# Half of an attention low part moved from VectorE to GpSimd, its scale folded into the exponential, and narrower reuse waits for one tile pool

## The chip, the cores and the metric

The kernel runs on one core of a Trainium2 chip. The metric is the device time of one execution in microseconds (us). The comparison is between the median of several executions of the kernel before and after one change; one further execution of each is profiled.

## The reference

The layer normalizes x, then adds to x an attention block and a mixture of experts that both read the normalized x. All eight experts are taken for every token (K = E = 8), so the gate is a softmax over eight logits.

```python
B, S, D, H = 1, 2048, 448, 16          # attention; Dh = 28
B, S, D, F, E = 1, 2048, 448, 1792, 8  # experts
def _A_ref(x, wqkv, wo):
    q, k, v = ...                                    # (B, H, S, Dh) each
    scores = jnp.einsum("bhqd,bhkd->bhqk", q, k) * (Dh ** -0.5)
    p = _softmax(scores, axis=-1)
    o = jnp.einsum("bhqk,bhkd->bhqd", p, v)
    return ... @ wo
def _B_ref(x, w_gate, w1, w2):
    ...
    for e in range(E):
        h = _silu(xf @ w1[e]) @ w2[e]
        out = out + w * h
xn = _layernorm(x, axis=-1)
return x + _A_ref(xn, A_wqkv, A_wo) + _B_ref(xn, B_w_gate, B_w1, B_w2)
```

## The kernel before, in words

**Numbers as two halves.** Products that need more than one fp16 are done with a value split in two: a high part (the value rounded to fp16) and a low part (the value minus the high part, again fp16). High parts are made on ScalarE (ACT), low parts on VectorE (DVE) or GpSimd (POOL), and TensorE (PE) adds up high times high, high times low and low times high.

**Two streams and one phase ahead of them.** `phase0` normalizes x, makes Q and K (written to the scratch tensor `qk` in DRAM) and V (`vs`). Then two streams run interleaved to the end. `moe` takes 24 groups of expert columns: `hidden` (L1062 and, for the last 64 rows of the contraction, `tails` L1070, four products in quarters of the array) makes z, `silu` makes t = silu on ACT and DVE (L1104, L1107), its high part hh on ACT (L1110) and its low part hl on POOL in two pieces of 256 columns (L1114), and `summed` (L1131) multiplies by the second weight and adds to `acc` on DVE (L1143). The weights' low parts are on POOL as well (L556, L574).

**Attention** takes 16 heads x 16 tiles of 128 queries, each tile in two halves j of 1024 keys, 512 halves in all. For a half, `score` makes the products (L1222) into the one PSUM slot of tag "s", DVE takes the row maximum mx (L1226), `expo` on ACT makes nm = -c mx (L1237, 128x1) and pf = exp(c s + nm) (L1238, f32), and `halves` makes ph = fp16(4096 pf) on ACT (L1247) and pl = 4096 pf - ph on DVE (L1250). `turn` transposes ph and pl by DMA on SP's queue (L1266) into th and tl. Every four tiles `weigh` multiplies tl by V (L1300, four products in column strips of 32) and th by V (L1307); small sums follow on POOL and DVE. Every fourth head `project` multiplies by wo (L1407). The next score product into slot "s" has to wait until the exponential has read the slot: score, maximum, nm, exponential, score is a loop that runs 512 times.

**What sets the order.** `Plan` records jobs with an estimated duration and then places them one by one with a list scheduler: for each engine the job with the lowest due time that is ready by the estimates. The order found is written out as each engine's program, in that order; on the chip each engine and SP's queue take it in order and wait on semaphores. For PE the scheduler ranks down work that has been ready for less than SURE = 2500 ns, and it keeps products in quarters or strips together (KEEP, HOLD), since it counts FORM = 95 ns for entering such a block. A DVE job marked `lock` and a POOL job are counted as excluding each other (SHARED).

**Pools.** `Pools` opens a pool "p0" for the tiles of `phase0`; when the last job that uses it has been placed, it closes p0 and opens "ap" over the same memory, for the attention's tiles (V, K, Q, pf, ph, pl, th, tl and others). In SP's queue the first job of "ap" is the load of head 0's V, then follow the loads of its K and Q.

Of the kernel before, what the change touches and what calls it, by code (L numbers as in the profile page):

```python
# [2 lines left out]

# [6 lines left out]
F32 = mybir.dt.float32  # L10
F16 = mybir.dt.float16
I32 = mybir.dt.int32
AF = mybir.ActivationFunctionType
ALU = mybir.AluOpType
# [4 lines left out]
P = 128  # L19
# [7 lines left out]
C = 512  # L27
# [7 lines left out]
P_SCALE = 4096.0  # L35
# [25 lines left out]
class Plan:  # L61
# [15 lines left out]
    def add(self, eng, ns, fn, v, r=(), w=(), size=0, after=(), lock=False, land=0, form=0, pace=0, rush=False):  # L77
        j = Job()
        j.lock, j.land, j.form, j.pace, j.rush, j.at = lock, land, form, pace, rush, 0
        j.eng, j.ns, j.fn, j.v, j.seq, j.size = eng, ns, fn, v, len(self.jobs), size  # L80
        j.then = []
        deps = set(after)
        for k in r:
            if k in self.wrote:
                deps.add(self.wrote[k])
        for k in w:
            if k in self.wrote:
                deps.add(self.wrote[k])
            deps.update(self.read.get(k, ()))
        for k in r:  # L90
            self.read.setdefault(k, []).append(j)
        for k in w:
            self.wrote[k], self.read[k] = j, []
        j.wait = len(deps)
        for d in deps:
            d.then.append(j)
        j.bufs = []
        for k in (*r, *w):
            b = k[0] if isinstance(k, tuple) else k
            if isinstance(b, Buf) and b not in j.bufs:  # L100
                j.bufs.append(b)
                b.users += 1
        j.many = sum(isinstance(k, Buf) and k.pool == "ps" for k in w) > 1
        j.frees = next((k for k in r if isinstance(k, Buf) and k.pool == "ps"), None) if eng != "PE" else None
        self.jobs.append(j)
        return j
# [204 lines left out]
class Pools:  # L311
# [17 lines left out]
    def issued(self, j):  # L329
        if any(b.pool == "p0" for b in j.bufs):  # L330
            self.left -= 1
            if not self.left:
                self.ctx.__exit__(None, None, None)
                del self.have["p0"]
                self.ctx = self.tc.tile_pool(name="ap", bufs=1)
                self.have["ap"] = self.ctx.__enter__()
                self.have["tl"] = self.ring

# [5 lines left out]
def block_kernel(ctx, tc, x, wqkv, wo, w_gate, w1, w2, out):  # L344
    nc = tc.nc
# [35 lines left out]
    shift = mp.tile([P, NT], F32, name="shift")  # L381
    cexp = mp.tile([P, 1], F32, name="cexp")
    cneg = mp.tile([P, 1], F32, name="cneg")
    sc_o = mp.tile([P, 1], F32, name="sc_o")
    inv_o = mp.tile([P, 1], F32, name="inv_o")

# [789 lines left out]
    def attention(at):  # L1176
# [53 lines left out]
        def expo(i, j, v):  # L1230

            PR[i, j] = p = buf("ap", [P, 2 * C], F32, f"pf{i}_{j}", tag="pf", bufs=RF)
            s, m, n = sc.pop((i, j)), mx[i // NB * NB], i % NB
            nm = buf("ap", [P, 1], F32, f"nm{i}_{j}", tag="nm", bufs=4)

            def powers():
                nc.scalar.activation(nm(), m()[:, n, j : j + 1], AF.Copy, scale=cneg)  # L1237
                nc.scalar.activation(p(), s(), AF.Exp, bias=nm(), scale=cexp)  # L1238

            add("ACT", 1532, powers, v, r=[s, (m, n, j), "cexp"], w=[p, nm])  # L1240

        def halves(i, j, v):
            p = PR.pop((i, j))
            h, l = PF[i, j] = [
                buf("ap", [P, 2 * C], F16, f"p{a}{i}_{j}", tag=f"p{a}", bufs=n) for a, n in (("h", RPH), ("l", RPL))
            ]
            add("ACT", 1052, lambda: nc.scalar.activation(h(), p(), AF.Copy, scale=P_SCALE), v, r=[p], w=[h])  # L1247
            add(
                "DVE", 1212,
                lambda: nc.vector.scalar_tensor_tensor(l(), p(), P_SCALE, h(), op0=ALU.mult, op1=ALU.subtract), v,  # L1250
                r=[p, h], w=[l], lock=True,
            )

        def turn(i, j, v):
            q = i % NB
            if not q and not j:
                PT[i] = [], []
            hs, ls = PT[i - q]
            h, l = PF.pop((i, j))
            if not j:  # L1260
                hs.append(buf("ap", [P, NKT, P], F16, f"th{i}", tag="th_", bufs=TH))
                ls.append(buf("tl", [P, NKT, P], F16, f"tl{i}", tag="tl", bufs=TL))
            th, tl, ks = hs[q], ls[q], slice(j * NKT // 2, (j + 1) * NKT // 2)
            for b, p, out in (((th, j), h, lambda: th()[:, ks]), ((tl, j), l, lambda: tl()[:, ks])):
                add(
                    "SP", 1290, lambda out=out, p=p: nc.sync.dma_start_transpose(out(), p()), v, r=[p], w=[b],  # L1266
                    size=950, land=TURN,
                )

# [151 lines left out]
        for i, (h, t) in enumerate(TILES):  # L1421
            v = at(i)
# [36 lines left out]
YPARTS = (0, 2), (2, 5)  # L1459
SPARE, SPINS, KAT, ONACT, NAT = 9, 6, -500, 'vqk', (-2000, -250, 0, 0)  # L1460
PACE, HOLD, CUT = 3500, 8000, 256
LANDQ, LANDX, SPK = 7500, 8500, -300
TURN, TURN_S, LOAD, MXS, SCM, LK, LQ = 5500, 4500, 4500, 4700, 4600, 3000, 2600
# [23 lines left out]
```

## Time and profile before

| | us |
|---|---|
| median of 3 executions | 2631.62 (2630.65 to 2634.79) |
| the profiled execution's own time | 2626.93 |
| its span, first to last instruction | 2625.1 |
| PE busy | 2609.3 (99%) |
| DVE busy | 2138.0 (81%) |
| ACT busy | 2115.9 (81%) |
| POOL busy | 1380.7 (53%) |

Busy time of an engine is the time in which at least one of its instructions runs. Matmuls overlap, and the end of each is modelled, so a busy PE may still be slower than it could be: the distance between two starts tells its pace. Granted clock 1.00 is 2.4 GHz, and 0.50 is 1.2 GHz. A stage's wait is read in the view of waits, which names who ended an engine's idle time.

### The profile page before, as it was taken

The page shows a single profiled execution, that of the slowest core. Times are in us where ns is not written, and L with a number is a line of the kernel's source. Part 1 is how long each engine was busy: PE and PEld are TensorE (multiplying, and loading weights), DVE is VectorE, ACT ScalarE, POOL GpSimd, SP SyncE. Part 2 cuts the span into 40 slices and gives each one's busy share as a digit, 9 for nine tenths or more (in the row PEclk, how much of TensorE's full clock was granted, in tenths as well). Part 3 has the DMA queues.
Part 4 walks back from the last instruction along what each step waited for, and adds up shares of the span by engine and source line. Part 5 has one row for each costly group of instructions (what it writes and reads, how often), then busy time and mean ns, then how long its engine had stood idle before and what let it go on. Part 6 is the DMA issues. An engine that isn't in the chain of part 4 may idle for free.

```text
span 2625.1 us, 49947 instructions
## 1 busy us (share of the span) xinstructions
PE 2609.3 (99%) x17851; PEld 1283.5 (49%) x17851; DVE 2138.0 (81%) x2832; ACT 2115.9 (81%) x3134; POOL 1380.7 (53%) x1915
## 2 busy tenths in 40 slices
PE   9999999999999999999999999999999999999999
PEld 4444444544445444444454444445444444444544
DVE  8478888788988888888888788978888788877873
ACT  6488898778987889878888788887898788887862
POOL 2255475535654456555546455554565455655542
PEclk9999999999999999999999999999999999999999
DMA  7568888888887888688796787968887788867751
GB/s 233 176 125 160 172 153 145 144 146 154 153 154 147 156 158 169 125 154 152 140 174 120 144 147 145 166 118 149 168 159 129 136 144 159 165 122 132 136 103 63
DMA packets 1221465, 386.84 MB, mean 147 GB/s; under 512 B 1156832, under 2 KB 1203296, under 8 KB 1221216
## 3 DMA queue, kind: packets, MB, share of 16 engines
q1 hardware_dynamic: 1220656, 383.63, 77.2%
q8 instruction: 140, 2.29, 0.4%
q14 instruction: 109, 0.89, 0.1%
q10 hardware_dynamic: 560, 0.02, 0.0%
HBM read 85.11 MB, written 15.23 MB: 38 GB/s over the span
## 4 chain that ended last, share of the span: by engine, by line
PE 93%; DVE 3%; ACT 2%; DMA 1%; issue 1%; SPq 0%; DVEq 0%; ACTq 0%
PE banks L1131 37%; PE banks L1062 34%; PE banks L1222 8%; PE banks L1307 4%; PE banks L893 3%; PE banks L1300 2%; PE banks L1070 2%; PE banks L916 1%; PE banks L1407 1%; DVE mx L1226 1%; DVE pl L1250 1%; ACT pf L1238 0%; DMA tl<-pl 0%; DMA scmg<-mxs 0%; ACT ph L1247 0%
## 5 line engine op out<-in xcount | busy, mean ns | idle before, releaser
L1114 POOL TENSOR_TENSOR hl<-t,hh 128x256 f16<-128x256 f32 x896 | 718.2, 822 | 647.2 <-ACT hh L1110 613.2
L1062 PE MATMUL banks<-xa,w 128*128 128x512 f16 x3136 | 974.9, 380 | 0.0
L1131 PE MATMUL banks<-w,hh 128*128 128x448 f16 x3584 | 970.6, 352 | 1.8 <-DVE t L1107 1.8
L1226 DVE TENSOR_REDUCE mx<-banks 128x1 f32<-128x1024 f32 x512 | 624.2, 1219 | 133.3 <-PE banks L1222 123.4
L1250 DVE SCALAR_TENSOR_TENSOR pl<-pf,ph 128x1024 f16<-128x1024 f32 x512 | 683.9, 1337 | 41.8 <-ACT ph L1247 38.5
L1062 PEld LDWEIGHTS <-w 128*128 128x128 f16 x4480 | 425.8, 97 | 531.3 <-issue 39.6
L1131 PE MATMUL banks<-w,hl 128*128 128x448 f16 x1792 | 631.3, 352 | 0.0
L1238 ACT ACTIVATE pf<-banks,nm,cexp 128x1024 f32<-128x1024 f32 x512 | 616.9, 1205 | 17.1
L1247 ACT ACTIVATE ph<-pf 128x1024 f16<-128x1024 f32 x512 | 538.2, 1051 | 5.6 <-DMA th<-ph 1.2
L1131 PEld LDWEIGHTS <-hh 128*128 128x128 f16 x3584 | 346.3, 98 | 343.5 <-issue 5.4
L1062 PE MATMUL banks<-xb,w 128*128 128x512 f16 x1344 | 509.1, 379 | 0.0
L1107 DVE SCALAR_TENSOR_TENSOR t<-t,banks 128x512 f32<-128x512 f32 x448 | 297.6, 681 | 96.8 <-ACT t L1104 95.5
L1237 ACT ACTIVATE nm<-mx,cneg 128x1 f32<-128x1 f32 x512 | 148.7, 290 | 270.5 <-DVE mx L1226 268.3
L1143 DVE SCALAR_TENSOR_TENSOR acc<-banks,gwe,acc 128x448 f32<-128x448 f32 x384 | 258.9, 678 | 126.3 <-PE banks L1131 125.4
L1104 ACT ACTIVATE t<-banks,the 128x512 f32<-128x512 f32 x448 | 295.3, 681 | 60.9 <-PE banks L1070 38.9
L1110 ACT ACTIVATE hh<-t 128x512 f16<-128x512 f32 x448 | 268.0, 622 | 59.6 <-PE banks L1131 54.3
L1222 PE MATMUL banks<-K,Q 112*128 112x512 f16 x1024 | 306.2, 380 | 4.3 <-DMA K<-qk 2.1
L1131 PEld LDWEIGHTS <-hl 128*128 128x128 f16 x1792 | 174.8, 98 | 164.2
L556 POOL TENSOR_TENSOR w<-r,w 128x256 f16<-128x256 f32 x224 | 176.1, 805 | 101.8 <-ACT w L552 101.8
L574 POOL TENSOR_TENSOR w<-r,w 128x224 f16<-128x224 f32 x224 | 150.4, 691 | 78.2 <-ACT w L571 72.5
L1222 PEld LDWEIGHTS <-Q 112*128 112x128 f16 x1024 | 94.5, 98 | 108.8 <-issue 20.3
L1307 PEld LDWEIGHTS <-th 128*128 128x128 f16 x4096 | 127.2, 96 | 27.9 <-issue 1.3
(154 smaller groups left out, 1839.5 us busy)
## 6 DMA issues: line engine op xcount, KB each, us to landing
r<-in_B_w_dram SPq DMA_DIRECT2D x48, 448.0 KB
r<-in_B_w_dram SPq DMA_DIRECT2D x48, 320.0 KB
th<-ph SPq DMA_TRANSPOSE x512
tl<-pl SPq DMA_TRANSPOSE x512
K<-qk SPq DMA_DIRECT2D x128, 56.0 KB
Q<-qk SPq DMA_DIRECT2D x256, 28.0 KB
r<-in_B_w_dram SPq DMA_DIRECT2D x24, 256.0 KB
r<-in_B_w_dram SPq DMA_DIRECT2D x32, 160.0 KB
```

Source lines behind the costliest of these rows:

```text
L1062: nc.tensor.matmul(z(), rows(w)[:, blk, :], xx, start=(i == 0 and not late), stop=(i == NTERM - 2 and late))
L1104: add("ACT", 680, lambda: nc.scalar.activation(t(), z(), AF.Tanh, scale=th_()[:, 0:1]), v, r=[z, th_], w=[t])
L1107: lambda: nc.vector.scalar_tensor_tensor(t(), t(), 1.0, z(), op0=ALU.add, op1=ALU.mult),
L1110: add("ACT", 620, lambda: nc.scalar.activation(hh(), t(), AF.Copy), v, r=[t], w=[hh])
L1114: nc.gpsimd.tensor_tensor(hl()[:, cs], t()[:, cs], hh()[:, cs], ALU.subtract)
L1131: nc.tensor.matmul(y()[:, 0:D], a, wv, start=(i == 0 and u == 0), stop=(i == g - 1 and u == 2))
L1143: lambda: nc.vector.scalar_tensor_tensor(acc[:, n, :], y()[:, 0:D], gb()[:, n : n + 1], acc[:, n, :], op0=ALU.mult, op1=ALU.add),
L1222: nc.tensor.matmul(b()[:, cs], q()[:, q0 : q0 + P], k()[:, cs], start=True, stop=True)
L1226: "DVE", 1220, lambda: nc.vector.tensor_reduce(m()[:, n, j : j + 1], b(), op=ALU.max, axis=AX.X), v,
L1238: nc.scalar.activation(p(), s(), AF.Exp, bias=nm(), scale=cexp)
L1247: add("ACT", 1052, lambda: nc.scalar.activation(h(), p(), AF.Copy, scale=P_SCALE), v, r=[p], w=[h])
L1250: lambda: nc.vector.scalar_tensor_tensor(l(), p(), P_SCALE, h(), op0=ALU.mult, op1=ALU.subtract), v,
```

## The change

Three things are changed together. nm becomes `Identity(-c mx + log 4096)`, with the constant in a tile `lift` as bias, so that pf comes out multiplied by 4096 and ph is a plain rounding of it. The low part is then pf - ph, a `tensor_tensor`: for the first half of every tile (j = 0) it stays one instruction on DVE, for the second half (j = 1, by `MIX`) it becomes two instructions of 512 columns on POOL (`CUTP`), and the transpose of that half waits for both pieces. And the pool "ap" is opened with `reuse_waits="tile"`: each of its tiles waits only for those users of p0 whose bytes it takes over.

```diff
-                self.ctx = self.tc.tile_pool(name="ap", bufs=1)
+                self.ctx = self.tc.tile_pool(name="ap", bufs=1, reuse_waits="tile")
...
+    lift = mp.tile([P, 1], F32, name="lift")
+    nc.vector.memset(lift, math.log(P_SCALE))
...
-                nc.scalar.activation(nm(), m()[:, n, j : j + 1], AF.Copy, scale=cneg)
+                nc.scalar.activation(nm(), m()[:, n, j : j + 1], AF.Identity, bias=lift, scale=cneg)
                 nc.scalar.activation(p(), s(), AF.Exp, bias=nm(), scale=cexp)
...
-            add("ACT", 1052, lambda: nc.scalar.activation(h(), p(), AF.Copy, scale=P_SCALE), v, r=[p], w=[h])
-            add(
-                "DVE", 1212,
-                lambda: nc.vector.scalar_tensor_tensor(l(), p(), P_SCALE, h(), op0=ALU.mult, op1=ALU.subtract), v,
-                r=[p, h], w=[l], lock=True,
-            )
+            add("ACT", 1052, lambda: nc.scalar.activation(h(), p(), AF.Copy), v, r=[p], w=[h])
+            if (2 * i + j) % MIX[1] not in MIX[0]:
+                add("DVE", 1212, lambda: nc.vector.tensor_tensor(l(), p(), h(), ALU.subtract), v, r=[p, h], w=[l], lock=True)
+                return
+            for k in range(2 * C // CUTP):
+
+                def low(cs=slice(k * CUTP, (k + 1) * CUTP)):
+                    nc.gpsimd.tensor_tensor(l()[:, cs], p()[:, cs], h()[:, cs], ALU.subtract)
+
+                add("POOL", POOL_NS(CUTP), low, v, r=[p, h], w=[(l, k)])
...
+CUTP, MIX = 512, ((1,), 2)
```

The estimate for nm and the exponential together (1532 ns) is left as it was. Since the jobs' engines change, the scheduler finds another order for the whole of the two streams; the number of instructions of PE, ACT's work and the two table loads of ACT stay as they were.

SP's queue before, from the last writes of Q and K by `phase0` (`qk<-qh`, `qk<-ql`) to the first loads of the attention (V0, K0_0 and Q0_0 of head 0), with the semaphores that each row waits for; the program's DMAs raise the eight semaphores DMAHW0 to DMAHW7 in turn as they land, so these make eight groups:

```order
L389 DMA mxs_69<-mxr1_1322 128x2 [waits DMAHW2_49,DVE_49]
L389 DMA qk_68<-qh3_6_1320 128x512 [waits DMAHW3_49,Activation_49]
L389 DMA qk_68<-ql3_6_1328 128x512 [waits DMAHW4_49,DVE_49]
L389 DMA V0_1347<-vs_70 128x1024 [waits DMAHW4_49,DMAHW5_49,DMAHW3_49,DMAHW6_49,DMAHW1_49,DMAHW7_49,DMAHW0_49,PE_49]
L389 DMA K0_0_1353<-qk_68 28x1024 x4
L389 DMA Q0_0_1374<-qk_68 28x512 [waits DMAHW2_49]
L389 DMA Q0_0_1374<-qk_68 28x512 x2
L389 DMA Q0_0_1374<-qk_68 28x512 [waits DMAHW5_49]
```

The same place now:

```order
L392 DMA mxs_69<-mxr1_1324 128x2 [waits DMAHW2_49,DVE_49]
L392 DMA qk_68<-qh3_6_1322 128x512 [waits DMAHW3_49,Activation_49]
L392 DMA qk_68<-ql3_6_1330 128x512 [waits DMAHW4_49,DVE_49]
L392 DMA V0_1349<-vs_70 128x1024 [waits DMAHW5_49]
L392 DMA K0_0_1355<-qk_68 28x1024 [waits DMAHW6_49]
L392 DMA K0_0_1355<-qk_68 28x1024 [waits DMAHW7_49]
L392 DMA K0_0_1355<-qk_68 28x1024 [waits DMAHW0_49]
L392 DMA K0_0_1355<-qk_68 28x1024 [waits DMAHW1_49]
L392 DMA Q0_0_1376<-qk_68 28x512 [waits DMAHW2_49]
L392 DMA Q0_0_1376<-qk_68 28x512 [waits DMAHW3_49]
L392 DMA Q0_0_1376<-qk_68 28x512 [waits DMAHW4_49]
L392 DMA Q0_0_1376<-qk_68 28x512 [waits DMAHW5_49]
```

The order of the rows is the same; the load of V0 waited for seven groups of DMAs and for PE and now waits for one group, and each of the eight loads behind it waits for the previous DMA of its own group, the last write to `qk` (DMAHW4) among them for the third piece of Q0_0.

POOL before, around the first low parts hl of column block 1 of expert group 2, with the small sums of attention tiles 20 to 23 (lw20, u20) between:

```order
L574 TENSOR_TENSOR w2_3_0_4314<-r2_3_3658,w2_3_0_4314 128x224 x2
L1336 TENSOR_TENSOR lw20_4359<-lw20_4359 128x8x29
L1340 TENSOR_TENSOR lw20_4359<-lw20_4359,c20_4155 128x8x29
L1114 TENSOR_TENSOR hl2_0_1_4423<-t2_0_1_4367,hh2_0_1_4411 128x256
L1344 TENSOR_TENSOR u20_4220<-u20_4220,lw20_4359 128x8x29
L1114 TENSOR_TENSOR hl2_0_1_4423<-t2_0_1_4367,hh2_0_1_4411 128x256
```

POOL now, around the same hl:

```order
L1257 TENSOR_TENSOR pl24_1_4359<-pf24_1_4322,ph24_1_4341 128x512 x2
L1117 TENSOR_TENSOR hl2_0_1_4381<-t2_0_1_4336,hh2_0_1_4357 128x256 x2
L559 TENSOR_TENSOR w1_3_4_4238<-r1_3_3299,w1_3_4_4238 128x256 x2
L1117 TENSOR_TENSOR hl2_1_1_4415<-t2_1_1_4352,hh2_1_1_4395 128x256 x2
L1117 TENSOR_TENSOR hl2_2_1_4438<-t2_2_1_4379,hh2_2_1_4426 128x256 x2
L1257 TENSOR_TENSOR pl25_1_4461<-pf25_1_4411,ph25_1_4436 128x512 x2
```

The low parts of attention tiles 24 and 25 (pl24_1, pl25_1), which stood on DVE, stand in POOL's row ahead of and behind the experts' hl.

On PE the order holds blocks of products in quarters or strips (L1070, L1300 before) that are entered from full products: 145 such blocks before, 149 now.

## Rows read from the trace of the kernel before

**Rows 1.** The page's busy time by engine (busy us, share of the span, instructions), the first row of its chain that ended last, and that chain's shares of the span by line, from the view of the chain in order of time.

```profile
PE 2609.3 (99%) x17851; PEld 1283.5 (49%) x17851; DVE 2138.0 (81%) x2832; ACT 2115.9 (81%) x3134; POOL 1380.7 (53%) x1915
...
PE 93%; DVE 3%; ACT 2%; DMA 1%; issue 1%; SPq 0%; DVEq 0%; ACTq 0%
...
by line: PE banks L1131 37.0%; PE banks L1062 34.1%; PE banks L1222 8.2%; PE banks L1307 3.9%; PE banks L893 2.5%; PE banks L1300 2.3%; PE banks L1070 2.1%; PE banks L916 1.3%; PE banks L1407 1.2%; DVE mx L1226 0.9%; issue 0.7%; DVE pl L125
```

**Rows 2.** The view of waits for PE alone, whole span: who waited for whom, us in total, times, longest us.

```profile
PE banks L956 <- DMA acc<-in_A_x_dram: 4.6, 1, 4.6
PE banks L1222 <- DMA K<-qk: 2.1, 1, 2.1
PE banks L1131 <- DVE t L1107: 1.8, 1, 1.8
PE banks L1222 <- ACT pf L1238: 1.7, 3, 1.3
PE banks L956 <- ACT xn L790: 1.0, 1, 1.0
PE banks L1307 <- DMA th<-ph: 0.3, 1, 0.3
```

**Rows 3.** The chain that ended last in order of time, 115 to 137 us: start us, us, what. SPq is SP's queue.

```profile
120.87 3.91 DMA qk<-ql
...
125.05 0.32 SPq L389
...
128.00 0.39 SPq L389
...
128.74 0.31 SPq L389
...
130.53 0.56 DMA K<-qk
131.08 1.00 PE banks L1222 x2
```

**Rows 4.** The view of stretches: from:to in us and length, busy us of PE, PEld, DVE, ACT, POOL (instructions), granted clock of PE, share of DMA, GB/s.

```profile
126.00:131.08 5.08, 2.98 (x15) 1.21 (x14) 0.84 (x2) 2.03 (x4) 3.85 (x6) 1.00 0.50 144
131.08:134.45 3.37, 3.37 (x9) 1.13 (x10) 1.89 (x2) 1.35 (x3) 0.00 (x0) 0.50 0.39 87
134.45:140.00 5.55, 5.55 (x28) 2.28 (x27) 2.87 (x5) 3.79 (x6) 1.30 (x2) 1.00 0.74 184
```

**Rows 5.** The timeline of PE around one block of products in quarters: start us, us, engine, line, operation.

```profile
123.20 0.59 PE L1062 MATMUL banks<-xa,w 128*128 128x512 f16 x2
123.73 0.39 PE L1070 MATMUL banks<-xa,w 64*128 64x512 f16 x1
...
123.96 0.38 PE L1070 MATMUL banks<-xa,w 64*128 64x512 f16 x1
...
124.27 0.39 PE L1062 MATMUL banks<-xa,w 128*128 128x512 f16 x1
124.49 0.38 PE L1062 MATMUL banks<-xb,w 128*128 128x512 f16 x1
```

**Rows 6.** Groups of instructions with shapes kept apart: line, engine, operation, out<-in, shapes, count | busy us, mean ns of one | idle us before them and what ended it. First DVE, then POOL, then ACT.

```profile
L1250 DVE SCALAR_TENSOR_TENSOR pl<-pf,ph 128x1024 f16<-128x1024 f32 x512 | 683.9, 1337 | 41.8 <-ACT ph L1247 38.5 <-ACT c L1313 1.4 <-DMA tl<-pl 1.0
L1226 DVE TENSOR_REDUCE mx<-banks 128x1 f32<-128x1024 f32 x512 | 624.2, 1219 | 133.3 <-PE banks L1222 123.4 <-ACT ph L1247 5.9 <-ACT t L1104 1.2
L817 DVE TENSOR_TENSOR tb<-xn,ta 128x448 f16<-128x448 f32 x8 | 5.0, 621 | 9.8 <-ACT ta L815 9.8
L410 DVE TENSOR_REDUCE mx<-r 128x1 f32<-128x1280 f32 x32 | 47.3, 1477 | 1.8 <-DMA r<-in_B_w_dram 1.8
L410 DVE TENSOR_REDUCE mx<-r 128x1 f32<-128x896 f32 x32 | 34.5, 1079 | 1.9 <-DMA r<-in_B_w_dram 1.9
...
L705 POOL TENSOR_TENSOR WA<-rqk,WA 128x448 f16<-128x448 f32 x4 | 4.1, 1036 | 11.2 <-DMA rwo<-in_A_wo_dram 6.0 <-DMA acc<-in_A_x_dram 5.1
...
L1237 ACT ACTIVATE nm<-mx,cneg 128x1 f32<-128x1 f32 x512 | 148.7, 290 | 270.5 <-DVE mx L1226 268.3
L570 ACT ACTIVATE r<-r,scog 128x448 f32<-128x448 f32 x112 | 73.4, 656 | 0.0
L790 ACT ACTIVATE xn<-acc,shift,rstd 128x448 f32<-128x448 f32 x15 | 10.6, 761 | 7.4 <-DVE tb L817 4.4 <-DVE shift L778 1.0 <-POOL WA L705 1.0
```

**Rows 7.** The views of two lines: the low part pl on DVE, and the experts' low part hl on POOL (durations min/median/max in ns), what hl waited for longest (us, times), and who waited for hl.

```profile
L1250 DVE SCALAR_TENSOR_TENSOR pl<-pf,ph x512: 1209/1224/1790, 138.2 to 2543.7; 128x1024 f16<-128x1024 f32 x171
...
L1114 POOL TENSOR_TENSOR hl<-t,hh x896: 658/671/1766, 126.3 to 2610.7; 128x256 f16<-128x256 f32 x180
...
  ACT hh L1110: 613.2, 199
...
  ACT t L1104: 3.0, 3
```

**Rows 8.** Timelines of ACT and PE where an exponential ends and the next score product starts, at the first and the last of the 44 places (of 511) where less than 0.1 us lies between.

```profile
215.35 1.20 ACT L1238 ACTIVATE pf<-banks,nm,cexp 128x1024 f32<-128x1024 f32 x1
...
216.65 0.60 PE L1222 MATMUL banks<-K,Q 112*128 112x512 f16 x2
...
2451.73 1.21 ACT L1238 ACTIVATE pf<-banks,nm,cexp 128x1024 f32<-128x1024 f32 x1
...
2452.99 0.38 PE L1222 MATMUL banks<-K,Q 112*128 112x512 f16 x1
```

More of the change, by code (lines that the diff above doesn't have):

```diff
@@ L2 @@
 import heapq
+import math
 import concourse.bass as bass
@@ L1265, in turn @@
                 add(
-                    "SP", 1290, lambda out=out, p=p: nc.sync.dma_start_transpose(out(), p()), v, r=[p], w=[b],
+                    "SP", 1290, lambda out=out, p=p: nc.sync.dma_start_transpose(out(), p()), v, r=[p] if p.tag == "ph" else [p, *((p, k) for k in range(2 * C // CUTP))], w=[b],
                     size=950, land=TURN,
```

## Prediction

> **What bounds the kernel now.** I read the busy times first, then the chain that ended last, then the waits of PE, then the one place where PE waits long. PE is busy for 2609.3 of 2625.1 us, and the chain is PE for 93% [rows 1]: nothing can be won here but what PE loses, and the change takes no instruction from PE. The view of waits gives all that PE loses to others: 4.6 + 2.1 + 1.8 + 1.7 + 1.0 + 0.3 = 11.5 us [rows 2]. Of these 4.6 and 1.0 (L956) lie ahead of the two streams, where the change alters nothing. So 5.9 us are left, with what the clock loses behind a wait, against which every new wait counts in full. DVE and ACT stand at 81%, POOL at 53% [rows 1]; what moves between them is worth nothing by itself. Only a wait that reaches PE is.
>
> **The pool's waits.** PE's longest wait in the streams is for the first attention loads: it is idle for 2.10 us until 131.08 [rows 2, 3], so it was ready at 128.98. Right behind it PE is granted 0.50 for 3.37 us, in which it is busy all the time, and 1.00 again after that [rows 4]: at half pace these 3.37 us do the work of 1.69, so 1.7 us go there. The wait and the clock cost 3.8 us together. Why the loads are late is in SP's queue: the last write of `qk` is issued at 120.87 (0.38 long) and lands 3.91 us later, at 124.78; only then V0's load goes, at 125.05 [rows 3], since it waits for all of p0's DMAs, and K0_0 and Q0_0 stand behind it. Now V0 waits for one group of DMAs. At best the whole row of loads moves up to the end of that issue, 121.25, by 3.8 us, and the products could start at 127.3. Against this stands that each load now waits for its own group: the third piece of Q0_0 waits for the write that lands at 124.78. It was issued at 128.00 [rows 3], so it comes 3.2 us earlier, and the products could start at 127.9. Both ends lie ahead of 128.98, so I take the whole 3.8 us off. Next late after that is ordinary work: the scores that follow wait for the slot, not for loads.
>
> **The low part on two engines.** DVE loses 256 instructions of 1337 ns [rows 6], 342 us, and falls to about 1796 us (68%). The 256 that stay become a plain `tensor_tensor`: 621 ns for 448 columns, and 1477 - 1079 = 398 ns more for 384 columns of a reduction, 1.04 a column, give 621 + 576 x 1.04 = 1.22 us [rows 6], the same as the 1224 ns of the old form [rows 7]. POOL gains 512 pieces. A low part of 256 columns takes 671 ns [rows 7], one of 448 takes 1036 [rows 6], 1.90 ns a column; a piece of 512 is then 1036 + 64 x 1.90 = 1158 ns, and 512 of them are 593 us. POOL comes to 1974 us, 75%. None of this lies on PE's path as long as the hl behind the pieces are in time: PE never waited for POOL [rows 2], and POOL idled 613 us in front of hl for want of hh [rows 7]. The transpose of a second half now waits for two pieces in line, 2.3 us where it was 1.2, behind which SP's queue stands; four tiles are weighed together, and PE waited for transposes 0.3 us in all [rows 2]. I cost this part at 0, with its loss among the rivals. The plain rounding of ph costs the same as the scaled one, and `lift` is set once ahead of everything: 0.
>
> **nm with a bias tile.** This term stands on a path. `Identity` with scale and bias tiles takes 761 ns on 448 columns, `Copy` with a scale tile alone 656 [rows 6]: a second tile as operand costs 0.105 us, so nm goes from 290 to about 395 ns, and ACT from 2115.9 to 2170 us (83%), hidden. But nm is in the loop score, maximum, nm, exponential, score, and the planner's estimate doesn't know of it. How often does that loop bind PE? By the chain, DVE's maximum has 0.9% of 2625.1 us, 23.6 us, or 19 maxima of 1219 ns [rows 1, 6]: 19 x 0.105 = 2.0 us. The bounds: 0, if the order found now leaves more room, and 44 x 0.1 = 4.4 us, since at 44 of 511 places the next score starts less than 0.1 us behind the exponential: from 215.35 + 1.20 to 216.65 at the first, from 2451.73 + 1.21 to 2452.99 at the last [rows 8]. I take 2.0, because the chain counts only the loops that had no other slack.
>
> **The new order of PE.** It enters blocks in quarters or strips 149 times, before 145. The second product ahead of such a block starts at 123.20 + 0.22 = 123.42 (full products start 0.22 apart, 124.27 to 124.49), the block at 123.73, 0.31 later; behind it 123.96 to 124.27 is again 0.31 [rows 5]. So a block costs 2 x 0.09 = 0.18 us, and four more 0.7 us. The bounds are 0 (fewer blocks follow straight on another) and 0.7; I take 0.7. The remaining waits in the streams (1.8 for t, 1.7 for the exponential, 0.3) are accidents of one order and will stand elsewhere in the new one; I leave them at their sum.
>
> **The sum.** -3.8 + 2.0 + 0.7 = -1.1 us. The profiled execution took 2626.93 us, 4.7 less than the median of 2631.62; its waits are applied to the median: 2631.6 - 1.1 = 2630.5 us, and with the bounds of nm (0 to 4.4) and the blocks (0 to 0.7) 2627.8 to 2632.9.
>
> **Rivals.** *The waits in the streams go too.* DVE loses 342 us of 2138, and PE's wait for t was one for DVE, so the room could take the 1.8 and the 1.7 away, with nm free: 2631.6 - 3.8 - 3.5 + 0.7 = 2625.0. For it: DVE's maxima start sooner. Against it: ACT gets fuller, and 2 of the 5.9 us hung on it.
>
> *POOL takes the wait's place, slower.* hl stands behind pieces of pl in one row. Two pieces (2.3 us) and one DVE low part that holds the port (1.2 us) delay an hl by 3.5 us; the planner holds some 2.5 us ready for PE (SURE), so 1.0 us of PE is idle each time. POOL and the DVE's remaining low parts together, were they never side by side, are 1974 + 256 x 1.22 = 2287 us, 87% of the span, so this must be a matter of single crowded places. From 7 of them on the kernel is slower by over 0.2%; eight give 2638.5. That the two engines exclude each other is seen in the rows: pl takes 1224 ns as a rule and up to 1790, hl 671 and up to 1766 [rows 7], each less than the other's length more. The Trainium skill (SBUF — State Buffer, "SBUF: two separate sides") calls this an exclusive lock of a port pair that is held for a whole instruction; the trace agrees by these maxima. The Trainium skill (GPSIMD Engine Reference, "Engine selection") speaks against the whole move: it wants two-input elementwise work on VectorE, with GpSimd about 2x slower; the rows say 2 x 1158 against 1224 ns, 1.9x, and it would cost only where POOL is waited for.
>
> *The pool's change does nothing for PE.* V0's load might share its way with the late writes and land no earlier than 3.7 us (125.05 to 128.74, the last piece of Q0_0) behind 124.78; that last piece waits for V0's group. Then the first product stays within 0.3 us of where it was, and 2631.6 + 2.0 + 0.7 = 2634.3 is left. Against it: V0's load would stand 3.8 us ahead in the queue.
>
> **How the numbers follow.** The forecast has 0.50, the waits that go too 0.23, POOL 0.17, the pool's change without effect 0.10. 0.2% is 5.3 us, about what a measurement of this kernel can tell from no change: faster means under 2626.4, slower over 2636.9. Faster: the second case and a little of the first's lower end, 0.25. Slower: POOL's, 0.17. The rest, 0.58, is the same. The range reaches from just under the second case, 2624.5, to 2638.0, which leaves out the worse half of POOL's case and little below; the forecast's own range is 2627.8 to 2632.9.
>
> **What would show it.** Right: PE has no wait near 129 us and its granted clock stays at 1.00 there; nm near 395 ns; the pieces on POOL near 1.16 us and POOL at about 75%, DVE near 68%; small waits of PE for the exponential in greater number. Wrong: rows of PE waiting for POOL's hl, or for the transposes of tl; a wait for K or Q still at 129 us; nm still at 290 ns.

## The result, and the profile after

The changed kernel takes 2653.53 us (median of 5 runs, 2652.06 to 2657.81), the kernel before 2631.16 us beside it (5 runs, 2628.0 to 2634.79). The ratio is 1.0087, 95% interval 1.0076 to 1.0097: the change costs 22.4 us. The forecast was 2630.5 with a range of 2624.5 to 2638.0, so it was wrong: too low by 23 us. It had counted differences of up to 0.2% as no change, and the changed kernel is slower by more than that. The profiled execution has a span of 2650.3 us, 25.2 more than before.

In the lines of the changed kernel the score product is L1225, the maximum mx L1229, nm L1240, the exponential L1241, ph L1250, pl L1252 on DVE and L1257 on POOL, hl L1117, and the transposes L1273.

Busy time by engine after, from the page; it answers to [rows 1]:

```profile
PE 2618.9 (99%) x17851; PEld 1283.1 (48%) x17851; DVE 1862.6 (70%) x2577; ACT 2162.0 (82%) x3134; POOL 1834.7 (69%) x2427
```

No engine but PE is near its limit. PE itself does the same 17851 products and is busy for 9.6 us longer, and its time without work grows by 25.2 - 9.6 = 15.6 us. A product's row lasts 380 ns though full products start 220 ns apart [rows 5], so a start that is late by less than some 160 ns (an estimate, 380 - 220) shows as longer busy time and not as a wait. That small delays stand in the 9.6 us is borne out below, by two runs with the same order of PE (e3 and e6).

Waits of PE after (who waited for whom, us in total, times, longest us); they answer to [rows 2]:

```profile
PE banks L1225 <- ACT pf L1241: 19.3, 27, 3.8
PE banks L959 <- DMA acc<-in_A_x_dram: 4.6, 1, 4.6
PE banks L959 <- ACT xn L793: 1.2, 1, 1.2
PE banks L1134 <- DVE t L1110: 0.5, 1, 0.5
PE banks L1065 <- DVE t L1110: 0.3, 1, 0.3
```

The wait of 2.1 us for K is gone, as forecast, and the wait for t is 0.8 us where it was 1.8. In their place the score waits for the exponential 27 times and 19.3 us; before it was 3 times and 1.7 us [rows 2]. POOL doesn't appear.

Groups of the moved work after (busy us, mean ns of one | idle us ahead of them and what ended it); the DVE and ACT groups of [rows 6] answer to them:

```profile
L1257 POOL TENSOR_TENSOR pl<-pf,ph 128x512 f16<-128x512 f32 x512 | 594.1, 1177 | 240.9 <-ACT ph L1250 162.9 <-DMA tl<-pl 43.5 <-issue 15.7
L1240 ACT ACTIVATE nm<-mx,lift,cneg 128x1 f32<-128x1 f32 x512 | 195.7, 382 | 236.3 <-DVE mx L1229 234.7
```

A piece on POOL takes 1177 ns on the mean and nm 382 ns: the durations came out about as forecast (1158 and 395).

Waits of ACT, then of POOL, after:

```profile
ACT ph L1250 <- POOL pl L1257: 22.0, 11, 4.8
ACT ph L1250 <- DMA th<-ph: 6.0, 3, 4.8
```

```profile
POOL pl L1257 <- DMA tl<-pl: 43.5, 25, 5.5
```

ACT's wait for pl is new, and so is POOL's for tl: before, pl stood on DVE and waited for tl 1.0 us in all [rows 6], and ACT waited in front of ph for this alone:

```profile
ACT ph L1247 <- DMA th<-ph: 1.2, 2, 0.6
```

How such a wait gets to PE is seen at PE's longest one. Timeline after, all engines, 579 to 594 us (start us, us, engine, line, operation, in brackets the idle time ahead of it and who ended it); SPq is SP's queue, where the us of a transpose is its issue:

```profile
579.39 1.06 ACT L1250 ACTIVATE ph<-pf 128x1024 f16<-128x1024 f32 x1 [0.67 <-POOL pl L1257]
...
580.41 1.24 SPq L1273 DMA_TRANSPOSE tl<-pl  x1
...
582.01 1.20 ACT L1241 ACTIVATE pf<-banks,nm,cexp 128x1024 f32<-128x1024 f32 x1
582.17 1.47 DVE L1252 TENSOR_TENSOR pl<-pf,ph 128x1024 f16<-128x1024 f32 x1 [0.61 <-DMA tl<-pl]
...
585.74 2.28 POOL L1257 TENSOR_TENSOR pl<-pf,ph 128x512 f16<-128x512 f32 x2 [3.18 <-DMA tl<-pl]
...
586.18 1.22 DVE L1229 TENSOR_REDUCE mx<-banks 128x1 f32<-128x1024 f32 x1
...
588.06 1.06 ACT L1250 ACTIVATE ph<-pf 128x1024 f16<-128x1024 f32 x1 [4.84 <-POOL pl L1257]
...
592.04 0.38 ACT L1240 ACTIVATE nm<-mx,lift,cneg 128x1 f32<-128x1 f32 x1
592.45 1.21 ACT L1241 ACTIVATE pf<-banks,nm,cexp 128x1024 f32<-128x1024 f32 x1
...
593.71 0.59 PE L1225 MATMUL banks<-K,Q 112*128 112x512 f16 x2 [3.84 <-ACT pf L1241]
```

Read from the top: ph is ready at 580.45, but POOL can't begin its low part until 585.74, because the buffer of pl (a ring of two) is still being read by the transpose that was issued at 580.41. POOL's two pieces end at 588.02. Until then ACT stands in front of the next ph, whose buffer (also a ring of two) POOL is reading: 4.84 us idle. That is the buffer of the half just before, and not that of the last but one, whose low part DVE had finished at 582.17 + 1.47 = 583.64. It is so in 10 of the 11 waits of ACT for pl, with 21.4 of the 22.0 us: ph of a first half waits for POOL's pl of the second half just before it, 1.0 to 5.0 us after DVE was through with the buffer of the last but one. Why the two buffers aren't taken in turn here isn't shown. The maximum for the next half is ready at 586.18 + 1.22 = 587.40, but nm stands in ACT's row behind that ph and behind the experts' weights, and starts at 592.04. The score's slot is free at 593.66, and PE has been idle for 3.84 us.

Stretches after, around this place (from:to in us and length, busy us of PE, PEld, DVE, ACT, POOL, granted clock of PE, share of DMA, GB/s):

```profile
583.00:589.90 6.90, 6.87 (x89) 3.37 (x88) 4.78 (x14) 2.03 (x4) 2.28 (x2) 1.00 0.51 82
589.90:594.94 5.04, 1.23 (x6) 0.58 (x6) 0.59 (x1) 4.98 (x9) 2.57 (x4) 1.00 0.92 175
594.94:598.36 3.42, 3.42 (x10) 1.21 (x8) 3.42 (x5) 3.39 (x6) 2.47 (x3) 0.50 0.79 155
```

Behind the wait PE is granted half the clock (1.2 GHz) for 3.42 us, which costs another 1.7. The half clock that followed the wait for K [rows 4] is gone with that wait.

### The profile page after: what moved, and what is told of

It is laid out like the page before. It is cut to its first block, busy times and chain, and to the rows that moved or that the text cites. A ratio compares the mean times of both kernels' runs of the same rounds, so it can differ in the third digit from the quotient of the medians.

```text
span 2650.3 us, 50122 instructions
## 1 busy us (share of the span) xinstructions
PE 2618.9 (99%) x17851; PEld 1283.1 (48%) x17851; DVE 1862.6 (70%) x2577; ACT 2162.0 (82%) x3134; POOL 1834.7 (69%) x2427
## 5 line engine op out<-in xcount | busy, mean ns | idle before, releaser
L1117 POOL TENSOR_TENSOR hl<-t,hh 128x256 f16<-128x256 f32 x896 | 654.2, 752 | 259.8 <-ACT hh L1113 259.1
L1229 DVE TENSOR_REDUCE mx<-banks 128x1 f32<-128x1024 f32 x512 | 624.5, 1220 | 231.9 <-PE banks L1225 203.1
L1257 POOL TENSOR_TENSOR pl<-pf,ph 128x512 f16<-128x512 f32 x512 | 594.1, 1177 | 240.9 <-ACT ph L1250 162.9
L1241 ACT ACTIVATE pf<-banks,nm,cexp 128x1024 f32<-128x1024 f32 x512 | 616.8, 1205 | 17.9
L1250 ACT ACTIVATE ph<-pf 128x1024 f16<-128x1024 f32 x512 | 538.0, 1052 | 36.1 <-POOL pl L1257 22.0
L1240 ACT ACTIVATE nm<-mx,lift,cneg 128x1 f32<-128x1 f32 x512 | 195.7, 382 | 236.3 <-DVE mx L1229 234.7
L1252 DVE TENSOR_TENSOR pl<-pf,ph 128x1024 f16<-128x1024 f32 x256 | 353.9, 1382 | 31.3 <-ACT ph L1250 23.8
L1225 PE MATMUL banks<-K,Q 112*128 112x512 f16 x1024 | 305.4, 379 | 20.9 <-ACT pf L1241 19.3
L559 POOL TENSOR_TENSOR w<-r,w 128x256 f16<-128x256 f32 x224 | 164.0, 753 | 45.6 <-ACT w L555 44.3
L1225 PEld LDWEIGHTS <-Q 112*128 112x128 f16 x1024 | 95.2, 98 | 137.1 <-issue 54.4
```

Of the source, the lines that this page charges most:

```text
L1117: nc.gpsimd.tensor_tensor(hl()[:, cs], t()[:, cs], hh()[:, cs], ALU.subtract)
L1225: nc.tensor.matmul(b()[:, cs], q()[:, q0 : q0 + P], k()[:, cs], start=True, stop=True)
L1229: "DVE", 1220, lambda: nc.vector.tensor_reduce(m()[:, n, j : j + 1], b(), op=ALU.max, axis=AX.X), v,
L1252: add("DVE", 1212, lambda: nc.vector.tensor_tensor(l(), p(), h(), ALU.subtract), v, r=[p, h], w=[l], lock=True)
L1257: nc.gpsimd.tensor_tensor(l()[:, cs], p()[:, cs], h()[:, cs], ALU.subtract)
```

## The experiments

Two theories were to be told apart: the longer nm makes the loop of score, maximum, nm and exponential too long for an order that was packed for 1532 ns; or the low parts on POOL delay the others. Four kernels take the change apart, and further ones ask why. The kernel before was run beside each group of them, at medians of 2629.5 to 2631.2 us, so a difference of under 2 us between two rows of the table isn't settled. In the last column are the places, of 511, where the next score starts less than 0.1 us behind the exponential, counted as in [rows 8]. PE takes its products in the same order in before, e1, e3, e6 and e7, and so it does in after and e2, and in e4 and e18; every other run has an order of its own. In e12, e17 and e19 one added line near the head shifts L numbers by one, and the spare work shifts later lines further.

| run | nm | pl of second halves | estimate ns | median us | ratio, 95% interval | tight places |
|---|---|---|---|---|---|---|
| before | 290 | DVE | 1532 | 2631.16 | 1 | 44 |
| after | 382 | POOL | 1532 | 2653.53 | 1.0087, 1.0076 to 1.0097 | 137 |
| e1_reuse_only | 290 | DVE | 1532 | 2626.10 | 0.9984, 0.9976 to 0.9993 | 42 |
| e6_nm_constant_low_on_dve | 290 | DVE | 1532 | 2624.87 | 0.9981, 0.9972 to 0.9990 | 37 |
| e3_low_on_dve | 382 | DVE | 1532 | 2637.92 | 1.0029, 1.0018 to 1.0040 | 135 |
| e2_nm_constant | 290 | POOL | 1532 | 2642.81 | 1.0043, 1.0031 to 1.0055 | 66 |
| e16_dve_nm_planned | 382 | DVE | 1627 | 2626.57 | 0.9989, 0.9980 to 0.9998 | 46 |
| e4_nm_planned | 382 | POOL | 1627 | 2630.38 | 1.0003, 0.9994 to 1.0013 | 47 |
| e18_pool_room | 290 | POOL | 1627 | 2629.79 | 0.9994, 0.9985 to 1.0003 | 24 |
| e12_pool_load | 290 | DVE, spare work on POOL | 1532 | 2642.04 | 1.0047, 1.0030 to 1.0063 | 48 |
| e19_load_room | 290 | DVE, spare work on POOL | 1627 | 2625.02 | 0.9977, 0.9968 to 0.9987 | 12 |

**The pool's waits alone.** The kernel before, and of the change only this:

```diff
-                self.ctx = self.tc.tile_pool(name="ap", bufs=1)
+                self.ctx = self.tc.tile_pool(name="ap", bufs=1, reuse_waits="tile")
```

> The kernel before with the pool's narrower reuse waits alone; every engine's order is that of before. Both theories (nm's 92 ns, or GpSimd late) leave this part as predicted: the wait for K at 129 us and the half clock behind it go, 3.8 us, 2631.2 - 3.8 = 2627.4 us. If instead the pool's waits had cost something, it would be at or above 2631.

2626.10 us, 4.4 less than the kernel before beside it. Waits of PE in the streams:

```profile
PE banks L1222 <- ACT pf L1238: 4.2, 5, 2.5
PE banks L1131 <- DVE t L1107: 2.0, 1, 2.0
```

No wait for K is left, and PE is busy in all of the 6.00 us from 125 to 131 at clock 1.00. The term of -3.8 lies within what the interval allows (-1.8 to -6.3). It is read from the medians alone: the two profiled executions are equally long (spans of 2625.3 and 2625.1 us), since in that of e1 the waits for the exponential come to 4.2 us and not 1.7, and another stretch of half clock, 3.4 us, stands at 598 us.

**The whole change with a short nm.** 4096 as a constant bias, not a tile:

```diff
-                nc.scalar.activation(nm(), m()[:, n, j : j + 1], AF.Identity, bias=lift, scale=cneg)
+                nc.scalar.activation(nm(), m()[:, n, j : j + 1], AF.Copy, bias=math.log(P_SCALE), scale=cneg)
```

> The changed kernel with log 4096 as a constant of a Copy in place of a bias tile of an Identity, so that nm takes some 290 ns again; the order of every engine stays that of the changed kernel. Theory nm (the 92 ns that the planner doesn't know of lengthen the score loop): most of the loss goes, 2630 us or less. Theory GpSimd (the low parts there come late, hold up ScalarE's ph by its two buffers, and so the exponential): the waits for the exponential stay, 2645 us or more.

2642.81 us: 10.7 less than after, still 12 more than before. Its group of nm:

```profile
L1240 ACT ACTIVATE nm<-mx,cneg 128x1 f32<-128x1 f32 x512 | 148.6, 290 | 260.6 <-DVE mx L1229 258.0
```

nm is back at 290 ns, so the `Identity` with a second tile as operand is what it paid 92 ns for; no run has the one without the other. The Trainium skill (ScalarE: Activation LUTs, "What ACT_TABLE_LOAD costs") gives about 93 ns for each operand of this kind, a pointer to a 128x1 tile; the trace agrees. Neither theory is enough alone.

**The low parts back on DVE.** The whole change but for the move:

```diff
-CUTP, MIX = 512, ((1,), 2)
+CUTP, MIX = 512, ((), 2)
```

> The changed kernel with every low part on VectorE (MIX empty); the order of TensorE is then that of before, nm is the Identity with two tiles (382 ns). Theory nm: still slow, 2640 us or more. Theory GpSimd: 2627 to 2631 us, since nothing of attention's low parts is on GpSimd; by the prediction's term of 2.0 us for nm 2629.4.

2637.92 us: 15.6 less than after. Then both edits together (e2's nm, e3's MIX):

> Every low part on VectorE and nm with the constant: of the change only the pool's waits, the folded scale and the plain tensor_tensor are left, in the order of before. Both theories: 2627.4 us, the same as with the pool's waits alone. The difference to the kernel with the Identity and the low part on VectorE is nm's price in the order of before: 2.0 us by the prediction, 10 us or more by theory nm.

2624.87 us, 5.6 less than before. From here the prices are read: the longer nm costs 13.1 us with pl on DVE (e3 - e6) and 10.7 with pl on POOL (after - e2); the low parts on POOL cost 17.9 with the short nm (e2 - e6) and 15.6 with the long one (after - e3). So there are two causes of similar size, and they nearly add up.

Where the 13.1 us go can be seen by laying PE's starts of e3 and e6 side by side, since their order is the same. The profiled executions differ by 13.1 us as well, and 12.4 of them arise at starts of the score product L1225, the one that waits for the exponential: in some 80 places, all but 5 of them by less than 0.4 us. PE's busy time is 9.0 us longer in e3 (2615.7 against 2606.7) for the same products. So what the longer nm costs is many exponentials that are a little late.

**Is it the loop, or ACT's row?** e6, with the same 92 ns put on ph, which is outside the loop (a zero tile as bias):

```diff
-    nc.vector.memset(lift, math.log(P_SCALE))
+    nc.vector.memset(lift, 0.0)
-            add("ACT", 1052, lambda: nc.scalar.activation(h(), p(), AF.Copy), v, r=[p], w=[h])
+            add("ACT", 1052, lambda: nc.scalar.activation(h(), p(), AF.Identity, bias=lift), v, r=[p], w=[h])
```

> The kernel of low parts on VectorE and nm by a constant (2624.9 us), with the same 92 ns that the Identity cost put on ph's rounding in place of nm: an Identity with a tile of zeros as bias, 512 times. ScalarE's work is then that of the kernel with the longer nm (2637.9 us), but the addition stands outside the loop score, maximum, nm, exponential, score. Theory loop (each loop 92 ns longer is what TensorE waits for): 2625 to 2628. Theory backlog (ScalarE, 81% busy, hands its lateness on from job to job until it idles, so that it doesn't matter which job is longer): 2634 or more.

2633.86 us (1.0012, 1.0003 to 1.0021), 9.0 more than e6; the tight places go from 37 to 93. Laid side by side as above, 6.9 of the 7.1 us between the profiled executions arise at the score product again. So a longer loop isn't needed for a price of this size: 512 instructions on ACT that are each 92 ns longer than the order was made for make the exponentials late outside the loop as well.

**Rings, and a control.** e2 with three buffers of pl (shown), or of ph. That needs room, so one buffer of the second weight's ring goes; the control gives up that buffer alone.

```diff
-RW1, RW2, RH, RF, RPH, RPL = 9, 9, 7, 3, 2, 2
+RW1, RW2, RH, RF, RPH, RPL = 9, 8, 7, 3, 2, 3
```

> The low part of second halves on GpSimd with nm by a constant (2642.8 us), and a third buffer for pl, so that GpSimd's pl needn't wait for the transpose of the pl two halves earlier (43 us of waiting in 23 places); the ring of w2 is 8 instead of 9 to make room, and the order is planned anew. Theory rings (transpose late, GpSimd held by pl's ring, ScalarE held by ph's ring, exponential late): 2630 or less. Theory port (VectorE and GpSimd hold each other up, whatever the buffers): 2640 or more.

> The same with the third buffer for ph in place of pl (w2's ring 8): ScalarE needn't wait for GpSimd's pl of two halves earlier (24 us of waiting in 12 places), but GpSimd still waits for the transposes. Theory rings: 2632 or less, since the link to the exponential is cut. Theory port: 2640 or more.

> The control for both: low part of second halves on GpSimd, nm by a constant, two buffers for ph and pl, w2's ring 8. All theories: 2643 us as with a ring of 9, within 4 us; if it is far below, then the new order and not the buffers explains what the two others show.

2651.50, 2655.05 and, the control, 2657.89 us. The missing weight buffer, with the new order that it brings, costs 15 us here, and against the control the third pl brings 6.4 us; the 2.8 of the third ph aren't clear of the noise. ACT's waits for pl in the control, with the third pl and with the third ph:

```profile
ACT ph L1250 <- POOL pl L1257: 25.0, 15, 3.4
ACT pf L1241 <- POOL pl L1257: 2.5, 3, 1.1
```

```profile
ACT pf L1241 <- POOL pl L1257: 2.6, 3, 1.8
ACT ph L1250 <- POOL pl L1257: 1.6, 2, 0.8
```

```profile
ACT pf L1241 <- POOL pl L1257: 16.1, 15, 2.6
```

The third pl takes nearly all of that wait away; with the third ph it moves to the exponential, whose pf (a ring of three) POOL is reading. The rings are a part of the price, and not most of it. The same weight buffer taken from e6:

> Every low part on VectorE, nm by a constant (2624.9 us), with w2's ring 8 instead of 9, planned anew. With GpSimd's low parts the same step cost 15 us (2642.8 to 2657.9). Theory order or ring: some 2640 here too. Theory GpSimd (only the fuller GpSimd makes the short ring and the order dear): 2625 to 2630.

2626.97 us (0.9989, 0.9979 to 0.9998): 2.1 more than e6. What costs 15 us with pl on POOL costs 2 without it; the kernel with pl on POOL is sensitive, the other is not.

**Is it one unlucky order?** An estimate 4 ns longer, 1532 to 1536, gives other orders of the same work: of e6, and of e2.

> Every low part on VectorE, nm by a constant (2624.9 us), and the planner's estimate of nm and exponential 4 ns higher, which changes nothing but the order that it finds. Theory order (the order of before was the lucky one of many): 2635 or more. Otherwise 2623 to 2630.

> Low part of second halves on GpSimd, nm by a constant (2642.8 us), with the same 4 ns: another order of the same work. Theory order: it can fall anywhere from 2625 to 2660, and by as much as the kernel with all on VectorE moves. Theory GpSimd: 2638 to 2650, while the other stays under 2630.

2624.50 us (0.9978, 0.9969 to 0.9988) and 2643.48 us (1.0052, 1.0037 to 1.0067): 19.0 between them, where e6 and e2 differ by 17.9. With these two estimates it isn't the luck of a single order.

**Load on POOL that nobody waits for.** e6 (pl on DVE) with three spare subtractions on POOL in each second half:

```diff
+    spare = mp.tile([P, 256], F16, name="spare")
...
+            if j:
+                for k in range(3):
+                    idle = lambda: nc.gpsimd.tensor_tensor(spare, xa[:, 0, 0:256], xb[:, 0, 0:256], ALU.subtract)
+                    add("POOL", POOL_NS(256), idle, v, r=[("done", i, j)])
```

> Every low part stays on VectorE and nm by a constant (2624.9 us), and GpSimd gets work that nobody waits for: with every second half three subtractions of 256 columns into a spare tile, 768 in all, some 520 us, known to the planner, so the order is planned anew. The result is that of the kernel. Theory handoff (what costs is that pl itself comes from GpSimd, later and in GpSimd's row, and holds the transposes, ph and the small sums): 2625 to 2632. Theory full GpSimd (its other work, hl and the small sums, comes late): 2640 or more. Theory order (any new order that nobody tuned costs this much): 2640 or more, too.

2642.04 us, 17.2 more than e6. Half of the low parts of e2 on POOL, MIX = ((1,), 4):

> nm by a constant; the low part on GpSimd for the second half of every other tile only, 128 of 512 in place of 256 (2642.8 us), none being 2624.9. A cost of each low part by itself (handoff) gives half of the 18 us: 2634. A cost of the row being full grows faster than the load: 2625 to 2630, with GpSimd near 60% busy.

2641.45 us (1.0046, 1.0031 to 1.0061). Half of the pieces cost as much as all of them (2642.81): the price doesn't go by their number. And e6 with seven memsets of `spare` in place of the subtractions, which read nothing:

> Every low part on VectorE, nm by a constant, and GpSimd work that nobody waits for, as in the run with 768 spare subtractions (2642.0 us), but as fillings of a spare tile, 7 of 256 columns with every second half, some 0.3 us each and 540 us in all, which read nothing. Theory port (subtractions that read both operands hold up VectorE's low parts, and are held up): the fillings don't, pl on VectorE is near 1224 ns by the mean, and 2624 to 2632 us. Theory full row: 2638 or more, since hl and the small sums wait in GpSimd's row either way.

2649.32 us (1.0077, 1.0061 to 1.0094), the dearest of the three. Groups of e17, then of e6:

```profile
L1257 DVE TENSOR_TENSOR pl<-pf,ph 128x1024 f16<-128x1024 f32 x512 | 670.2, 1310 | 60.8 <-ACT ph L1251 57.9 <-DMA tl<-pl 2.0 <-ACT r L574 0.2
...
L1254 POOL MEMSET spare<- 128x256 f16 x1792 | 558.2, 312 | 76.2
```

```profile
L1252 DVE TENSOR_TENSOR pl<-pf,ph 128x1024 f16<-128x1024 f32 x512 | 684.9, 1339 | 42.6 <-ACT ph L1250 37.5 <-DMA tl<-pl 3.8 <-ACT nm L1240 0.4
```

DVE's low parts aren't slowed by the memsets (1310 against 1339 ns), and yet the time is lost. So the two engines' excluding each other isn't needed for the loss: it is enough that POOL's row is fuller. One way by which it reaches ACT is seen: silu's t waits for the experts' hl on POOL, in e12 as in the first line, in e6 as in the second, and 9.7 us in e17. How much of the 17 to 24 us goes that way isn't shown.

```profile
ACT t L1108 <- POOL hl L1118: 19.0, 21, 2.4
```

```profile
ACT t L1107 <- POOL hl L1117: 3.0, 3, 1.7
```

**An order planned for a longer loop.** The whole change, and e3, with an estimate that has the longer nm in it:

```diff
-            add("ACT", 1532, powers, v, r=[s, (m, n, j), "cexp"], w=[p, nm])
+            add("ACT", 1627, powers, v, r=[s, (m, n, j), "cexp"], w=[p, nm])
```

> The changed kernel with the planner's estimate of nm and exponential raised by the Identity's extra time, 1532 to 1627 ns, so that the order is found with it. Theory estimate (what nm costs, it costs because the order is packed for a shorter one): the 10.7 us between 2653.5 and 2642.8 come back, 2640 to 2645. Theory full ScalarE (the 47 us of work cost what they cost in any order): 2650 or more.

> The same with every low part on VectorE, where other orders of the same work lay within 3 us: nm as Identity, known to the planner; 2637.9 us with the old estimate, 2624.9 with the short nm. Theory estimate: 2624 to 2630. Theory full ScalarE: 2634 or more.

2630.38 us and 2626.57 us. One number in the plan takes 23 us off the changed kernel, with the same instructions on the same engines, and 11 off e3. With this estimate POOL's pieces cost 3.8 us (e4 - e16), and e16 with its longer nm stands 1.7 over e6, which isn't settled.

To see whether it is the estimate's agreement with nm or the longer plan, the last two runs take the short nm with 1627: e2, and e12 with its spare load.

> e2_nm_constant (low part on GpSimd, nm 290 ns) with the loop's planned length raised from 1532 to 1627 ns, so that the order leaves about 95 ns of room in each loop. Theory A, the order packed with no room hands GpSimd's and the transposes' lateness on to PE: about as e4_nm_planned less some 2 us, so 2625 to 2630, against e2's 2642.8. Theory B, GpSimd's work slows the others by itself and e4 was a lucky order: 2638 or more. Theory C, it was only that nm and its estimate agreed in e4 and not in e2 (here they disagree the other way): 2632 to 2638.

> e12_pool_load (low part on VectorE, nm 290 ns, three spare subtractions on GpSimd per second half that nobody waits for) with the loop's planned length raised from 1532 to 1627 ns. Theory A, room in the plan takes the lateness up: 2625 to 2631, against e12's 2642.0. Theory B, a busier GpSimd costs by itself, whatever the order: 2638 or more.

2629.79 and 2625.02 us, 13.0 and 17.0 less than with 1532. e18 has the order of e4 with the short nm: there the longer nm costs 0.6 us (e4 - e18), which isn't clear of the noise. Waits of PE, of e18 and of e19, and busy time of e19:

```profile
PE banks L1225 <- ACT pf L1241: 8.1, 14, 2.0
```

```profile
PE banks L1226 <- ACT pf L1242: 3.5, 5, 1.6
```

```profile
PE 2609.9 (99%) x17851; PEld 1284.5 (49%) x17851; DVE 2173.5 (83%) x2833; ACT 2124.8 (81%) x3134; POOL 1992.8 (76%) x2683
```

POOL is fuller in e19 (1992.8 us, 76%) than in any other run, and the time is that of e6. So a busy POOL need not cost anything, but more work on POOL cost 16 us or more in each of the eight orders here that were planned with 1532 or 1536. The low parts on POOL keep a small price of their own in the wider order: e18 is 4.9 us over e6. ACT waits for POOL in e18 as follows:

```profile
ACT ph L1250 <- POOL pl L1257: 5.5, 4, 1.7
```

The best version is e6 or e14 (2624.87 and 2624.50 us): the pool's narrower waits, the scale folded into the exponential by a constant bias, and all low parts on DVE. It is 0.2% faster than the kernel before, clear of the noise; what the folded scale adds to the pool's waits (e1, 2626.10) isn't.

**What stays open.** The longer plan helps, but not simply by idle time left in each loop. From the start of nm to the end of the exponential it takes 1531 ns in e2 and 1624 in e4 (medians of 512 in the records), so both are planned to within 3 ns of what they take, and e4 is 12 us faster. What the wider orders have in common is that no place is bad. By the records of the kernels with more work on POOL, those planned with 1532 or 1536 (after, e2, e8, e9, e10, e11, e12, e15, e17) have one to three waits of PE over 2 us in the streams, and all but e10 one to four stretches at half clock; those planned with 1627 (e4, e18, e19) have neither. But one such wait stands in each of e1, e6 and e13 too (2.5, 2.0 and 2.7 us), which are fast, so bad places aren't the whole of it. And e4 and e18 share one order: with more work on POOL the wider estimate stands on two orders, both of them good, against eight of the narrower one. A third estimate wasn't tried, nor a kernel in which POOL's pieces share no buffers with ACT, nor one whose ph takes its two buffers strictly in turn.

## Why the prediction was wrong

**The step that failed: "None of this lies on PE's path as long as the hl behind the pieces are in time ... I cost this part at 0".** It asked only who waits for hl. It left out those who wait for the buffers: ACT's next ph waits until POOL has read the buffer that it is to fill, POOL's pl waits until a transpose has read its own, and all of these stand in rows that are worked off in order, ahead of nm and the exponential. And it left out that a fuller row of POOL costs even where nobody waits for the added work (e12 and e17, 17.2 and 24.5 us over e6). The term is 17.9 us (e2 - e6), not 0; in an order planned with 1627 it is 4.9 (e18 - e6). How the 17.9 divide among these waits stays open: the third buffers took only a part of it away. The prediction did name the transposes, and took PE's 0.3 us of waiting for them as their weight; in the changed kernel POOL waits for them 43.5 us, and ACT for pl 22.0.

**The second step that failed: nm at 2.0 with a bound of 4.4.** The duration was right (382 ns for 395), and so was the place. The count was wrong: "the chain counts only the loops that had no other slack" takes each loop for itself. e7 shows that 92 ns on another instruction of ACT's row are handed on too, so that places which had slack lose it: 37 tight places in e6 become 93 in e7 and 135 in e3. The term is 13.1 us (e3 - e6) with the old estimate; with 1627 it is 0.6 (e4 - e18) to 1.7 (e16 - e6), near the 2.0, but neither of these is clear of the noise. The sentence that the planner's estimate doesn't know of nm's length stood in the prediction, and its consequence wasn't drawn. All signs named for being right came, but for POOL's share of 69%, and none of those for being wrong: they looked at durations and at PE waiting for POOL or the transposes, and left open how much waiting for the exponential would be too much.

**The pool's waits** were right: -3.8 forecast, -4.4 measured (e1), with the wait for K and the half clock behind it gone. **PE's blocks** (+0.7) weren't measured apart; nothing here bears on them. **The waits in the streams unchanged**: wrong by the two steps above; the wait for t shrank from 1.8 to 0.8 us, that for the exponential grew from 1.7 to 19.3.

**The rivals.** "POOL takes the wait's place" had the sign and the engine, and a chance of 0.17. Its path was not what happened: PE never waited for hl, it waited for the exponential, and there were 27 waits and not eight. Its point that this must be a matter of single crowded places holds in part: the place at 589.9 us alone costs 3.84 + 1.7 = 5.5 us of the 22.4. That POOL and DVE exclude each other, which it counted on, isn't needed for a loss of this size (e17). "The waits go too" fell with e2, and "the pool's change does nothing" with e1.

**Sizes of lesser weight.** POOL came to 1834.7 us, not 1974, because its other work got shorter: 1834.7 - 594.1 = 1240.6 us against 1380.7 [rows 1]. That fits DVE holding fewer low parts beside it, but it wasn't tested. DVE came to 1862.6, not 1796. Its low parts account for 12 of these 67 us: they fell by 683.9 - 353.9 = 330.0 us, where the forecast took off 256 x 1337 ns = 342, and those that stay take 1382 ns on the mean. The rest wasn't traced.

```profile
L1252 DVE TENSOR_TENSOR pl<-pf,ph 128x1024 f16<-128x1024 f32 x256 | 353.9, 1382 | 31.3 <-ACT ph L1250 23.8
```

The sum as measured: -5.6 (e6 against the kernel before beside it: the pool's waits and the folded scale), +13.1 for nm, +17.9 for POOL, 25.4 in all, where the change as a whole costs 22.4; the two prices overlap by some 2 to 3 us.

## What to carry to other kernels

When PE is busy for 99% of the span, the order of the work is what there is to lose. Here a job that gets longer than the plan holds for it, or moves to another engine's row, was priced with all that stands behind it in that row and with the buffers it holds, not with its own wait. So change the planner's estimate together with the instruction (here 1532 to 1627 took back 11 to 23 us), and test a move with the estimate a little long as well. POOL's busy share told nothing of the price: 61% in e10 went with 16.6 us over e6, 76% in e19 with none.

## What the runs showed of the hardware that wasn't expected

In these runs PE's granted clock doesn't follow the length of an idle time alone. After 3.84 us of idle it fell to 0.50 (1.2 GHz) for 3.42 us (rows above, from 594.94), and in the kernel before after 2.10 us [rows 3, 4]; in the changed kernel 2.33 us of idle at 560 us, and in e10 3.06 us at 587 us, had no fall behind them and stayed at 1.00 (2.4 GHz). Even at the same place of the same order it goes both ways: 1.97 us of idle at 596 us in e1 had a fall behind them, 2.04 us at 598 us in e6 had none. Stretches of after, then of e10:

```profile
556.00:562.40 6.40, 4.07 (x21) 1.50 (x20) 1.55 (x3) 2.63 (x5) 5.88 (x9) 1.00 0.87 181
562.40:568.00 5.60, 5.60 (x26) 2.51 (x26) 4.87 (x8) 5.25 (x9) 3.48 (x6) 1.00 1.02 166
```

```profile
587.40:590.50 3.10, 0.04 (x1) 0.00 (x0) 3.00 (x11) 2.79 (x5) 1.39 (x3) 1.00 0.84 157
590.50:596.00 5.50, 5.49 (x53) 2.90 (x53) 4.14 (x5) 5.43 (x8) 4.56 (x7) 1.00 0.57 129
```

In the 25 us ahead of each of the six, PE's records show no other gap of over 0.2 us, so what PE did ahead of the idle time doesn't tell them apart either. What does isn't seen in these rows.
